# A planned attention and gated-MLP kernel: weight blocks in slice order, and new lengths in its planner

## The chip, the cores and the metric

The kernel runs on one core of one Trainium2 chip, and nothing else runs beside it. The metric is the time of one execution in microseconds (us), taken on the device; lower is better. Times of the planner stand in nanoseconds (ns), as in the code. The core's engines are called PE (matrix products), ACT, DVE and POOL in the profile's rows; SP only issues transfers. In the kernel's code PE, A, V, G and Q stand for PE, ACT, DVE, POOL and the queue that SP feeds.

## The reference

Attention in a band of 128 keys with 16 places for sink keys, of which 4 count, then a gated MLP on all heads together:

```python
batch, n_heads, seq, head_dim = (4, 8, 768, 64)
scores = scale * np.matmul(q, k.transpose(0, 1, 3, 2))
keep = is_sink | in_window          # pos < n_sink, or 0 <= rel < window
scores = np.where(keep, scores, -1000000000.0)
a = np.exp(scores - np.max(scores, axis=-1, keepdims=True))
a = a / (np.sum(a, axis=-1, keepdims=True) + 1e-09)
x = np.matmul(a, v)                 # then (B * S, H * D) = (3072, 512)
gate = 1.0 / (1.0 + np.exp(-(x @ w_gate)))      # w_gate, w_val: 512 x 1536
val = x @ w_val
out = gate * val @ w_out                        # w_out: 1536 x 512
```

The three weights are 64-bit floats on the host. They reach the chip as 64-bit words and are made into 32-bit floats there; the other arrays are 32-bit.

## The kernel before

**Attention.** A unit is one head, one batch and a stretch of 256 rows; there are 96 of them. A unit loads its q and k (`qkT`) and v (`vraw`, `vhl`), multiplies scores, masks and reduces them on DVE (`top`), takes the exponential on ACT (`exp`), scales by the sum (`share`, `mul` or `scale`, whichever engine takes it), turns the weights over on PE (`turn`), masks them into two parts on POOL (`split`, `rest_of`) and multiplies with v (`pv`). The first 20 units (`PLAIN`) do this in plain 32-bit products, the other 76 with numbers that are split into a high and a low half, so that PE can run its faster format. Four PSUM buffers (tag "a") serve the scores, the turned weights and the outputs of all units; an output of a plain unit stays in such a buffer until it has been copied out.

**The MLP.** The 12 stretches of 256 rows of x are grouped in 8 chunks, the last four of two stretches each ("pairs", which save products by sums of blocks). For every chunk the kernel goes through 12 slices of 128 of the 1536 inner columns: products with gate and value weights, tanh on ACT, product of both on DVE, split into `gh` and `gl`, and the product with the output weight, summed in PSUM. Chunk 0 (`feed_whole`) takes the decoded 32-bit weights as they are. While it runs, `halves` splits each weight block into a high half, which stays, and a low half, which `spare` writes to DRAM (`wlo_d`); `fetch` reads these back for all later chunks. `thirds` makes three more halves of each slice for the pairs.

**Weights.** For every slice `weights` loads three blocks of 128 x 512 64-bit numbers, 512 KB each (gate, value, output), through three buffers (`wst`), and `decode` makes 32-bit numbers of each with two steps on ACT (the second may go to DVE or POOL) and two on DVE. Gate and value blocks are cut out of 512 x 1536 matrices: each partition gets four rows of 1 KB. An output block has 4 KB in one row for each partition. Nothing is fetched from `wlo_d` before all blocks are decoded (`DECODED`).

**The order of the work.** Every step is written down as `plan.op(priority, ways, reads, writes)`, where `ways` lists the engines that could do it with the time in ns that the step would hold each of them. `Plan.run` plays the whole kernel through with these times when the kernel is built, gives each engine that comes free the ready step of lowest priority number (PE takes first what has been ready for a while, `SURE`), chooses buffers, and writes the instructions of each engine in the order so found. On the chip each engine works off its list in that order, whatever the real times are, and waits where an input is late. `LAT` (180 ns) is the time from a step's end to the start of a step on another engine that needs it, `NEXT` that on the same engine, `BULK`, 650 and 750 are parts of a transfer's time, `Port` marks steps of DVE and POOL that hold each other up. Until 130 us the planner puts in filler products (`warm`) where PE would otherwise be idle too long.

**The end.** Whether the fast path was valid is counted on the chip, and a branch at the end skips `general`, a slow path. `hint` places an instruction on PE, DVE and SP ahead of that branch that names its likely target; it stands in the last slice of the last chunk (`last_slice`).

## Time and profile before

| | |
|---|---|
| median of 3 runs | 771.19 us (770.46 to 771.49) |
| the profiled execution | 774.19 us |
| its span, first to last instruction | 772.5 us |
| busy: PE, DVE, ACT, POOL | 749.1, 607.5, 472.0, 506.1 us |
| mean granted clock of PE | 0.998 of 2.4 GHz |
| transfers | 184.45 MB, 75.9% of the 16 DMA engines' span |

The span lies 1.7 us under the profiled execution's own time, and that is 3.0 us over the median of the runs. "Busy" counts the time from an instruction's start to its modelled end, so that of two products that overlap in the pipeline the common part counts once. A share over the whole span is a mean over stages that differ; the rows further down take them apart.

### The profile page before, as it was taken

The page shows a single profiled execution, that of the slowest core. Times are in us where ns is not written, and L with a number is a line of the kernel's source. Part 1 is how long each engine was busy: PE and PEld are TensorE (multiplying, and loading weights), DVE is VectorE, ACT ScalarE, POOL GpSimd, SP SyncE. Part 2 cuts the span into 40 slices and gives each one's busy share as a digit, 9 for nine tenths or more (in the row PEclk, how much of TensorE's full clock was granted, in tenths as well). Part 3 has the DMA queues.
Part 4 walks back from the last instruction along what each step waited for, and adds up shares of the span by engine and source line. Part 5 has one row for each costly group of instructions (what it writes and reads, how often), then busy time and mean ns, then how long its engine had stood idle before and what let it go on. Part 6 is the DMA issues. An engine that isn't in the chain of part 4 may idle for free.

```text
span 772.5 us, 16296 instructions
## 1 busy us (share of the span) xinstructions
PE 749.1 (97%) x4986; PEld 674.9 (87%) x4986; DVE 607.5 (79%) x1782; ACT 472.0 (61%) x1338; POOL 506.1 (66%) x647
## 2 busy tenths in 40 slices
PE   7999999999999999999999999999999999999995
PEld 6866777998989999989999988999999999999995
DVE  5979988996999999969988889778999884433333
ACT  7879888765765777737666665457776652322221
POOL 3654676887999999937777977557976855321210
PEclk9999999999999999999999999999999999999999
DMA  6898987999999877677767777867697655677662
GB/s 165 222 297 250 323 263 234 376 307 311 342 294 319 284 220 207 200 252 231 233 224 225 242 233 222 246 196 251 193 306 249 196 159 178 217 240 211 198 205 86
DMA packets 120879, 185.57 MB, mean 240 GB/s; under 512 B 23248, under 2 KB 45264, under 8 KB 120784
## 3 DMA queue, kind: packets, MB, share of 16 engines
q1 hardware_dynamic: 120784, 184.45, 75.9%
q8 instruction: 42, 0.69, 0.4%
q14 instruction: 53, 0.43, 0.2%
HBM read 159.24 MB, written 25.17 MB: 239 GB/s over the span
## 4 chain that ended last, share of the span: by engine, by line
PE 61%; DVE 11%; DMA 6%; POOL 3%; ACT 2%; issue 2%; SPq 0%; ACTq 0%; POOLq 0%; DVEq 0%
PE m L620 34%; PE a L620 16%; PE o L620 11%; DVE ws L620 2%; DMA wst<-in_moe_w_gate_dram 1%; DMA out_dram<-w 1%; DVE P L620 1%; DVE th L620 1%; DMA vraw<-in_vt_dram 1%; DMA lo<-wlo_d 1%; DVE vhl L620 1%; POOL wt L620 1%; DVE hi L620 1%; DVE gl L620 1%; DVE xf L620 1%
## 5 line engine op out<-in xcount | busy, mean ns | idle before, releaser
L620 PE MATMUL m<-ws,ws 128*128 128x256 f32 x1536 | 290.0, 284 | 0.6 <-DVE th L620 0.2
L620 PE MATMUL m<-ws,lo 128*128 128x256 f32 x1344 | 288.6, 283 | 1.9 <-DMA lo<-wlo_d 1.3
L620 PEld LDWEIGHTS m<-ws,ws 128*128 128x128 f32 x1536 | 244.9, 189 | 13.1 <-DVE th L620 1.0
L620 PEld LDWEIGHTS m<-ws,lo 128*128 128x128 f32 x1344 | 215.0, 189 | 3.1 <-DMA lo<-wlo_d 2.3
L620 POOL TENSOR_SCALAR_AFFINE_SELECT wt<-wt 128x512 fp32r<-128x512 f32 (+3 forms) x192 | 125.9, 657 | 43.5 <-DVE wt L620 18.7
L620 POOL TENSOR_TENSOR gl<-th,gh 128x512 fp32r<-128x512 f32 (+1 forms) x34 | 38.2, 1122 | 99.6 <-ACT gh L620 82.7
L620 ACT ACTIVATE P<-P,negm_all 128x144 f32<-128x144 f32 x192 | 78.9, 412 | 28.7 <-DVE negm_all L620 26.8
L620 ACT ACTIVATE th<-m 128x256 f32<-128x256 f32 x96 | 36.6, 382 | 75.5 <-DVE th L620 71.9
L620 DVE TENSOR_TENSOR cv<-m,cv 128x256 f32<-128x256 f32 x96 | 40.2, 418 | 52.4 <-ACT cv L620 34.8
L620 ACT CAST gh<-th 128x512 fp32r<-128x512 f32 (+1 forms) x82 | 42.9, 523 | 55.3 <-DVE th L620 53.7
L620 POOL TENSOR_TENSOR ws<-ws,ws 128x512 fp32r<-128x512 f32 (+1 forms) x53 | 66.6, 1262 | 9.8 <-DVE ws L620 6.9
L620 PE MATMUL o<-ws,gh 128*128 128x512 f32 x168 | 67.6, 403 | 0.0
L620 PE MATMUL o<-ws,gl 128*128 128x512 f32 x168 | 66.2, 394 | 0.0
L620 PE MATMUL o<-lo,gh 128*128 128x512 f32 x168 | 65.8, 391 | 0.0
L620 DVE CUSTOM_DVE_ANT_0 P<-a,am 128x144 f32<-128x144 f32 x192 | 58.3, 306 | 8.8 <-PE a L620 2.2
L620 PE MATMUL a<-wt,vhl 128*128 128x256 f32 (+2 forms) x282 | 61.0, 327 | 1.8 <-POOL wt L620 1.6
L620 POOL TENSOR_TENSOR kl<-qkT,hi 128x400 fp32r<-128x400 f32 (+1 forms) x56 | 59.2, 1057 | 1.8
L620 PEld LDWEIGHTS a<-wt,vhl 128*128 128x128 f32 x282 | 47.3, 189 | 10.5 <-POOL wt L620 4.1
L620 ACT CAST hi<-qkT 128x656 fp32r<-128x656 f32 (+1 forms) x70 | 49.2, 703 | 10.9 <-PE a L620 10.0
L620 POOL TENSOR_TENSOR P<-P,rs 128x288 f32<-128x288 f32 x46 | 35.1, 764 | 29.8 <-DVE rs L620 26.2
L620 POOL TENSOR_TENSOR hi<-qkT,hi 64x256 fp32r<-64x256 f32 x53 | 41.2, 777 | 14.9 <-issue 4.9
L620 DVE COPY_PREDICATED a<-tri,a 128x128 f32<-128x128 int32 x160 | 45.4, 284 | 3.5 <-PE a L620 3.2
(146 smaller groups left out, 1735.5 us busy)
## 6 DMA issues: line engine op xcount, KB each, us to landing
lo<-wlo_d SPq DMA_DIRECT2D x396, 256.0 KB, 3.7
wlo_d<-ws SPq DMA_DIRECT2D x72, 256.0 KB, 4.3
qkT<-in_qk_dram SPq DMA_DIRECT2D x52, 328.0 KB, 4.1
qkT<-in_qk_dram SPq DMA_DIRECT2D x24, 264.0 KB, 3.5
wst<-in_moe_w_gate_dram SPq DMA_DIRECT2D x12, 512.0 KB, 4.8
wst<-in_moe_w_val_dram SPq DMA_DIRECT2D x12, 512.0 KB, 5.1
wst<-in_moe_w_out_dram SPq DMA_DIRECT2D x12, 512.0 KB, 5.4
out_dram<-w SPq DMA_DIRECT2D x20, 256.0 KB, 4.4
```

The costliest lines, as they stand in the source:

```text
L620: return lambda *a, **kw: tc.keep_in_program_order(op(*a, **kw))
```

## The change

- numpy puts the gate and value weights in the order slice, partition, block, column on the host, so that a block is loaded in rows of 4 KB; `weights` and the shapes taken from the arrays follow.
- The planner's times: ACT, POOL and some PE and DVE steps get shorter lengths; the time from a step's end to its reader is `AFTER` of the engine that did it and `TOLD` of the engine that reads, in place of `LAT`; a transfer takes `REACH` from its issue, its own time by `moved(packets, bytes)`, and `LANDED`; and the planner issues no transfer that would stand behind more than `QUEUED` ns of others.
- The eight loads of a batch's sink values write parts of a buffer, not all of it, in the planner's books.
- The copies of x of chunks 2 and 3 read `SPLIT`, which each of the 36 high halves of `halves` writes: the planner puts them behind all of these.
- `hint` is placed in the seventh slice of the last chunk (`NF - 6`) in place of the twelfth.

Three more hunks, each with one changed number of ns, and unchanged lines are left out.

```diff
@@ -57,13 +57,17 @@
-LAT = 180.0
-BULK = 620.0
-ISSUE = 550.0
+AFTER = dict(PE=163.0, V=75.0, A=100.0, G=35.0, Q=0.0)
+TOLD = dict(PE=54.0, V=35.0, A=35.0, G=77.0, Q=27.0)
+REACH = 1800.0
+LANDED = 600.0
+QUEUED = 4000.0
+SHARE = 1.6
+ISSUE = 480.0
...
-NEXT = dict(PE=0.0, V=60.0, A=60.0, G=60.0, Q=0.0)
+NEXT = dict(PE=0.0, V=10.0, A=25.0, G=0.0, Q=0.0)
@@ -86,6 +90,7 @@
+GUARD = 0
@@ -408,14 +413,19 @@
                     same = len(x.ways) == 1 and x.ways[0][0] == on
-                    x.ready = max(x.ready, now + (NEXT[on] if same else LAT))
+                    lat = AFTER[on] + TOLD[x.ways[0][0]]
+                    x.ready = max(x.ready, now + (NEXT[on] if same else lat))
-                        x.sure = max(x.sure, now + LAT + (SURE_D if o.dma else SURE))
+                        x.sure = max(x.sure, now + lat + (SURE_D if o.dma else SURE))
...
                 if free[e] > now:
+                    continue
+                if e == "Q" and dma_free > now + REACH + QUEUED:
+                    n += 1
+                    heapq.heappush(events, (dma_free - REACH - QUEUED, n, None))
@@ -440,7 +450,7 @@
-                        or any(slots[k][v - 1][1] + LAT + SURE > now for k, v in need.items())
+                        or any(slots[k][v - 1][1] + AFTER["V"] + TOLD["PE"] + SURE > now for k, v in need.items())
@@ -494,7 +504,7 @@
-                        port = now + ns + (70.0 if e == "V" else 0.0)
+                        port = now + ns + AFTER[e]
@@ -510,9 +520,8 @@
                     if o.dma:
-                        slow = BULK if o.dma > 1000.0 else 0.0
-                        dma_free = max(dma_free + o.dma, end + 650 + slow + o.dma)
-                        end = dma_free + 750
+                        dma_free = max(dma_free, now + REACH) + o.dma
+                        end = dma_free + LANDED
@@ -523,7 +532,7 @@
-                        x.due = max(x.due, end + LAT)
+                        x.due = max(x.due, end + AFTER[e] + TOLD[x.ways[0][0]])
@@ -561,14 +570,13 @@
-    w_gate, w_val, w_out = (
-        w.bitcast(I32).rearrange("r (c w) -> r c w", w=2) for w in (w_gate, w_val, w_out)
+    w_gate, w_val = (
+        w.bitcast(I32).rearrange("f p c (y w) -> f p c y w", w=2) for w in (w_gate, w_val)
+    w_out = w_out.bitcast(I32).rearrange("r (c w) -> r c w", w=2)
-    DM, DF, _ = w_gate.shape
+    NF, _, NC, _, _ = w_gate.shape
-    NC = DM // 128
-    NF = DF // 128
@@ -633,10 +641,13 @@
     def act(cols, psum=False):
-        return 120 + 0.9 * cols
+        return 28 + 0.93 * cols
     def pool(cols):
-        return Port(170 + 2.17 * cols)
+        return Port(135 + 2.17 * cols)
+
+    def moved(n, size):
+        return n * (9 + size / 27.0 + SHARE * size / 160.0)
@@ -836,7 +847,7 @@
-    WLO, LOADS, GROUPS, DECODED, READY, READY2 = (Fixed(None) for _ in range(6))
+    WLO, SPLIT, GROUPS, DECODED, READY, READY2 = (Fixed(None) for _ in range(6))
@@ -851,7 +862,7 @@
-                        u + 0.5, 91.0, lambda x=x, y=y, o=o: Q.dma_start(
+                        u + 0.5, moved(4, 256), lambda x=x, y=y, o=o: Q.dma_start(
@@ -862,9 +873,9 @@
-                u, 91.0, lambda o=o: Q.dma_start(
+                u, moved(8, 256), lambda o=o: Q.dma_start(
-                ), [READY2], [(raw, o)] + [VSHL[b, i] for i in range(2) if b and (b, i) in VSHL],
+                ), [READY2], [(raw, o)] + [(VSHL[b, i], o) for i in range(2) if b and (b, i) in VSHL],
@@ -880,11 +891,11 @@
-            u, 0.75 * n * R / D, lambda: Q.dma_start(out=qkT()[0:R, 0:n], in_=qk[b, h, 0:R, c0 : c0 + n]),
+            u, moved(R // 16, 4 * n), lambda: Q.dma_start(out=qkT()[0:R, 0:n], in_=qk[b, h, 0:R, c0 : c0 + n]),
...
-            u, 100.0 * L, lambda: Q.dma_start(
+            u, moved(8 * L, 256) if plain else moved(8, 256 * L), lambda: Q.dma_start(
@@ -969,12 +980,12 @@
-            plan.op(u, [("PE", 10 + (4 * n / 2.4 + 6 if plain else 2 * mac(n)), scores)], qk_reads, [sc, (P, t)], busy=0.5 if plain else 0.9)
+            plan.op(u, [("PE", (10 + 4 * n / 2.4 + 6 if plain else 249 if n > 256 else 177), scores)], qk_reads, [sc, (P, t)], busy=0.5 if plain else 0.9)
-                u, [("V", 260 if first else 535, top)],
+                u, [("V", 222 if first else 545, top)],
-            plan.op(u, [("A", 410, exp)], [], [(P, t), (rs, t)])
+            plan.op(u, [("A", 405, exp)], [], [(P, t), (rs, t)])
@@ -1000,16 +1011,16 @@
-                ("A", 200, lambda: A.activation(
+                ("A", 100, lambda: A.activation(
-                ("G", Port(213), guard(G)), ("V", Port(100), guard(V)),
+                ("G", Port(178), guard(G)), ("V", Port(75), guard(V)),
...
-            u, [("V", 110, lambda: V.reciprocal(out=rs()[:, 0:T], in_=rs()[:, 0:T]))], [], [rs]
-        )
-        plan.op(u, [("G", Port(660), share), ("A", 720, mul), ("V", Port(555), scale)], [rs], [P])
+            u, [("V", 75, lambda: V.reciprocal(out=rs()[:, 0:T], in_=rs()[:, 0:T]))], [], [rs]
+        )
+        plan.op(u, [("G", Port(621), share), ("A", 625, mul), ("V", Port(555), scale)], [rs], [P])
@@ -1070,7 +1081,7 @@
-        plan.op(u, [("PE", 30 + (T + plain) * 110, turn)], [P], [tp, wt], busy=0.45)
+        plan.op(u, [("PE", 20 + T * 60 + 190 * plain, turn)], [P], [tp, wt], busy=0.45)
@@ -1082,8 +1093,8 @@
-        plan.op(u, [("G", Port(180 + 0.9 * Z * (T - f) * 128), split)], [], [wt])
-        plan.op(u, [("G", Port(180 + 0.9 * Z * T * 128), rest_of)], [], [wt])
+        plan.op(u, [("G", Port(145 + 0.9 * Z * (T - f) * 128), split)], [], [wt])
+        plan.op(u, [("G", Port(145 + 0.9 * Z * T * 128), rest_of)], [], [wt])
@@ -1208,7 +1219,7 @@
                 hi, lo = lambda: H1()[:, i], lambda: L1()[:, i]
-                copy(u, W, hi, xv, read, [(H1, i), (L1, i)], plain)
+                copy(u, W, hi, xv, read + [SPLIT] * (ci > WHOLE + GUARD), [(H1, i), (L1, i)], plain)
@@ -1260,7 +1271,7 @@
-        plan.op(prio, [("Q", ISSUE, lambda: Q.dma_start(out=st(), in_=src))], [], [st], dma=1456.0)
+        plan.op(prio, [("Q", ISSUE, lambda: Q.dma_start(out=st(), in_=src))], [], [st], dma=moved(8, 8 * n * m))
@@ -1310,7 +1321,7 @@
-            decode(prio(), w[:, fs].rearrange("(c p) f w -> p c f w", p=128), whole)
+            decode(prio(), w[f], whole)
@@ -1318,7 +1329,7 @@
-            pr, 728.0, lambda: Q.dma_start(
+            pr, moved(8, 2048), lambda: Q.dma_start(
@@ -1326,7 +1337,9 @@
         hi, lo = slot(F32R, shape), slot(F32R, shape)
-        copy(pr, 512, hi, whole, [whole, *r], [hi, (lo, 0)], start=start)
+        copy(
+            pr, 512, hi, whole, [whole, *r], [hi, (lo, 0)] + [(SPLIT, (f, k))] * (k > 2), start=start
+        )
@@ -1388,7 +1401,7 @@
-            dma(ci, 728.0, lambda ot=ot, r=r: Q.dma_start(out=out[r : r + 128], in_=ot()), [ot])
+            dma(ci, moved(8, 2048), lambda ot=ot, r=r: Q.dma_start(out=out[r : r + 128], in_=ot()), [ot])
@@ -1464,7 +1477,7 @@
-                pr, 728.0, lambda x=x, k=k: Q.dma_start(
+                pr, moved(8, 2048), lambda x=x, k=k: Q.dma_start(
@@ -1636,6 +1649,8 @@
         gh, gl = gated(pr, 512, th)
+        if ci == len(CHUNKS) - 1 and f == NF - 6:
+            hint([gh], [th], [wol])
@@ -1662,7 +1677,6 @@
-        hint([(gh, 1)], [(th, 1)], [wol])
         high = gh, (lambda: woh()[:, 0], lambda: wol())
@@ -1797,6 +1811,8 @@
+    for name in ("moe_w_gate", "moe_w_val"):
+        made[name] = inputs[name].reshape(4, 128, -1, 128).transpose(2, 1, 0, 3)
```

## Rows read from the trace of the kernel before

**Rows 1.** Busy time by stage: length, time and count for each engine, clock, DMA share, GB/s.

```profile
0.00:20.00 20.00, 14.75 (x89) 12.99 (x90) 11.33 (x65) 15.05 (x45) 6.86 (x23) 1.00 0.64 162
20.00:140.00 120.00, 115.15 (x573) 88.61 (x572) 105.25 (x291) 104.11 (x223) 74.22 (x90) 1.00 0.89 272
140.00:340.00 200.00, 196.77 (x1386) 181.23 (x1385) 177.59 (x507) 131.30 (x412) 173.23 (x217) 1.00 0.87 283
340.00:480.00 140.00, 138.13 (x971) 128.19 (x969) 124.87 (x387) 88.85 (x274) 107.64 (x143) 1.00 0.72 228
480.00:760.00 280.00, 279.83 (x1957) 260.49 (x1956) 184.80 (x529) 130.68 (x382) 144.17 (x176) 1.00 0.69 214
760.00:772.50 12.50, 4.51 (x22) 3.39 (x20) 3.66 (x8) 2.00 (x5) 0.00 (x0) 0.87 0.24 89
```

**Rows 2.** The chain that ended last, 700 to 716 us: start, length, what.

```profile
710.80 1.43 PE m L620 x12
...
713.64 1.39 PE a L620 x6
```

**Rows 3.** Instruction groups of PE, shapes apart: count, busy us, mean ns, idle before.

```profile
L620 PE MATMUL m<-ws,ws 128*128 128x256 f32 x1536 | 290.0, 284 | 0.6 <-DVE th L620 0.2 <-ACT th L620 0.2
...
L620 PE MATMUL m<-ident 128*128 128x128 f32 x52 | 9.9, 317 | 1.4 <-POOL ident masks.py:199 1.4
```

**Rows 4.** Waits of PE: for whom, us in total, times, longest us.

```profile
PE a L620 <- POOL P L620: 3.3, 4, 1.9
PE a L620 <- POOL wt L620: 1.8, 4, 0.6
PE a L620 <- DMA qkT<-in_qk_dram: 1.6, 1, 1.6
```

**Rows 5.** Timeline of SP: first and last weight block, start and length of the issue.

```profile
8.71 0.59 SPq L620 DMA_DIRECT2D wst<-in_moe_w_gate_dram  x1
...
118.95 0.33 SPq L620 DMA_DIRECT2D wst<-in_moe_w_out_dram  x1
```

**Rows 6.** Two short stretches in the form of rows 1.

```profile
119.00:119.50 0.50, 0.50 (x2) 0.19 (x1) 0.31 (x1) 0.50 (x1) 0.00 (x0) 1.00 0.93 303
121.00:121.40 0.40, 0.40 (x3) 0.35 (x3) 0.40 (x2) 0.40 (x4) 0.04 (x1) 1.00 0.89 317
```

**Rows 7.** DMA issues of the page: count, KB each, median us from issue to landing.

```profile
lo<-wlo_d SPq DMA_DIRECT2D x396, 256.0 KB, 3.7
...
wst<-in_moe_w_gate_dram SPq DMA_DIRECT2D x12, 512.0 KB, 4.8
...
wst<-in_moe_w_out_dram SPq DMA_DIRECT2D x12, 512.0 KB, 5.4
out_dram<-w SPq DMA_DIRECT2D x20, 256.0 KB, 4.4
```

**Rows 8.** Instruction groups of POOL and ACT, shapes apart, columns as in rows 3.

```profile
L620 POOL TENSOR_SCALAR_AFFINE_SELECT wt<-wt 128x512 fp32r<-128x512 f32 x128 | 94.7, 741 | 19.5 <-DVE wt L620 14.7 <-DVE rs L620 1.4 <-ACT th L620 0.2
L620 ACT ACTIVATE P<-P,negm_all 128x144 f32<-128x144 f32 x192 | 78.9, 412 | 28.7 <-DVE negm_all L620 26.8 <-POOL wt L620 0.3
...
L620 ACT ACTIVATE th<-m 128x256 f32<-128x256 f32 x96 | 36.6, 382 | 75.5 <-DVE th L620 71.9 <-PE m L620 3.1
...
L620 POOL TENSOR_TENSOR P<-P,rs 128x288 f32<-128x288 f32 x46 | 35.1, 764 | 29.8 <-DVE rs L620 26.2 <-PE a L620 3.4
```

**Rows 9.** Waits of ACT, columns as in rows 4.

```profile
ACT w L620 <- DMA out_dram<-w: 9.1, 6, 2.7
```

**Rows 10.** Timelines of DVE and ACT: a copy of x, a high half.

```profile
93.96 0.41 DVE L620 CAST ws<-a 128x256 fp32r<-128x256 f32 x1
...
146.72 0.62 ACT L620 CAST ws<-ws 128x512 fp32r<-128x512 f32 x1
```

**Rows 11.** Timeline of SP at the end.

```profile
764.55 1.55 SPq L620 DMA_DIRECT2D out_dram<-xf  x1
```

**Rows 12.** DMA queues, 764.5 to 765.8 us: packets, MB, share of 16 engines.

```profile
q8 instruction: 1, 0.02, 5.6%
```

More of the change, by code (lines that the diff above doesn't have):

```diff
@@ L1025, in attend @@
             plan.op(
-                u, [("V", 180, lambda: V.transpose(
+                u, [("V", 160, lambda: V.transpose(
                     out=turned().rearrange("p t x -> p (t x)"),
@@ L1036, in attend @@
             plan.op(
-                u, [("G", Port(610), spread(G)), ("V", two(W), spread(V))], [turned, OWN], [sk]
+                u, [("G", Port(568), spread(G)), ("V", two(W), spread(V))], [turned, OWN], [sk]
             )
@@ L1279, in decode @@
                 )),
-                ("G", Port(1340.0), lambda: G.tensor_scalar(
+                ("G", Port(1305.0), lambda: G.tensor_scalar(
                     out=by(2), in0=by(1), scalar1=2.0**-13, scalar2=-8191.0 / 16384, op0=ALU.mult,
```

## The prediction

> **What bounds the kernel now.** I read the busy time by stage first, because the page's 97% for PE is an average. From 480 to 760 us PE stands still for 280.00 - 279.83 = 0.17 us: nothing there can be gained by another order [rows 1]. One pair slice in that stage is a fixed row of products at 1.43 / 12 = 0.119 us each and of output steps at 1.39 / 6 = 0.232 us each [rows 2]. Both rates are the same everywhere, and the change alters neither the count of the products nor their tiles, so PE's useful work is fixed. What can change is the time in which PE does nothing useful. The reader is to see five places [rows 1]: 5.25 us idle in the first 20 us; 4.85 us from 20 to 140; 3.23 us from 140 to 340; 1.87 us from 340 to 480; and 7.99 us from 760 to the end, after the last products. Then there are the filler products that keep PE warm, 9.9 us [rows 3]. An idle stretch costs a little more than it shows: a product counts as busy for 0.284 us [rows 3] where the next could have followed after 0.119, so each gap hides up to 0.165 us. So at most some 10 us between 20 and 480, a part of the start, and a part of the end are to be had, of 774.2 us for the profiled execution. The runs have a median 3.0 us lower (771.19 us); I make the sum on the profiled execution and carry the difference over.
>
> Who keeps PE waiting is the second view: POOL's scaling of P and its masking of wt, 5.1 us together, and one load of q and k with 1.6 us [rows 4]. The weight load path is the third: 36 blocks are issued between 8.71 and 118.95 us [rows 5], one per 3.1 us, through three buffers, so that a buffer takes 9.2 us for load and decoding. That path is slow, yet PE is 96% busy meanwhile (115.15 of 120 us) with attention and chunk 0; decoding sets PE's pace only where PE idles.
>
> **The layout.** A gate or value block is 512 KB, in 1 KB rows before and in 4 KB rows after, as the output weight's blocks are already. In a half microsecond filled with 1 KB rows the queue moved 303 GB/s at a share of 0.93; in a stretch of 4 KB rows alone 317 GB/s at 0.89 [rows 6]. At full share that is 326 and 356 GB/s, or 1.61 and 1.47 us for a block: 0.14 us saved. Eight such blocks go through each of the three buffers, so the last block could be decoded 8 x 0.14 = 1.1 us earlier. The other bound is the landing: blocks in 4 KB rows took 5.4 us from issue, gate blocks 4.8 [rows 7]; if it is the rows that make the 0.6 us, decoding ends 8 x 0.6 = 4.8 us later. I think it is the place (the output block usually stands behind the other two), and PE's own work covers 96% of the stage either way: 1.1 us becomes 0.04. I take 0 and keep -1.1 and +4.8, which hold if PE runs out of other work.
>
> The Trainium skill (DMA: Bandwidth & Descriptors, Specifications) gives 512 B as the smallest transfer for line rate, by which 1 KB rows lose nothing and the layout saves nothing; the two rates above differ by 9%, so the trace does not quite agree. By either the sum is the same, as I take 0.
>
> **The planner's lengths.** This part re-draws every engine's order, and carries nearly all that can happen. For a 256-column ACT step the planner before takes 120 + 0.9 x 256 = 350 ns, and 180 more until another engine sees it: 530. After, it is 28 + 0.93 x 256 = 266, then 100 + 35 = 135: 401. The trace shows such a step as 382 ns long [rows 8], so the new figure is the truer one, and ACT was charged about 0.13 us too much per step. Many copies may go to ACT or DVE, and with the old figure they went to DVE, which is busy 105.25 of 120 us from 20 to 140, against 104.11 for ACT, whose busy time counts the step's tail. With ACT cheaper, copies move off DVE. I take half of the 4.85 us of that stage: -2.4 us (bounds 0 and -4.85).
>
> For a 256 KB load the planner before has 550 + 650 + 728 + 750 = 2.68 us from issue to landing; after it has 1.8 + 0.84 + 0.6 = 3.24 us. The median of 396 such loads is 3.7 us, of the output's stores 4.4 us [rows 7], so loads are asked for earlier and stores are believed later. ACT now waits 9.1 us for such stores, up to 2.7 us at a time, at the chunks' ends [rows 9], with the later ACT steps queued behind it. Of the 5.1 us between 140 and 480 I take a third: -1.7 us (bounds 0 and -5.1). That a batch's sink loads are no longer planned one after another belongs to the same term. The new hold on the DMA queue (nothing is issued that would stand behind more than 4 us of transfers) acts mostly in the first 20 us, where a load of q and k stood behind weight blocks; the start also depends on filler, and I take 0 with bounds of half its idle time, -2.6 and +2.6.
>
> **The guard (SPLIT).** The copies of x of chunks 2 and 3 now wait for the last of 36 high halves. Before, the first copy of chunk 2 ran at 93.96 us; a high half of the 36 was still copied at 146.72 [rows 10]. The first two of these sums lie in PSUM, in two of the four "a" buffers, which score, transpose and output of all units share. If they are held for these 53 us, attention goes on with two. With 96 units in some 640 us about eight fall into that time, and if one ACT exponential of 0.41 us [rows 8] is no longer hidden in each, that is +3.3 us. In its favour: four weight buffers that chunk 2 took early stay free for the halves, which then end sooner. I take 0 (bounds 0 and +3.3).
>
> **The hint** moves from the last slice to five slices earlier, about 5 x 7.8 = 39 us [rows 2]. At the end the second output store's issue took 1.55 us on SP, where a usual one takes 0.33 [rows 5, 11], and in that stretch an instruction packet is in the trace [rows 12]; the last two stores are queued behind it. If the fetch falls elsewhere, 1.2 us go; if it falls on the last store, as much may come. I take half, -0.6 us (bounds -1.2 and +1.2).
>
> **Sum.** 0 - 2.4 - 1.7 + 0 + 0 - 0.6 = -4.7 us: 769.5 us for a profiled execution, 766.5 us for the median.
>
> **Rivals.** *Lengths too short (slower).* One mechanism: the new POOL figures are those of an undisturbed step. Scaling P is 621 ns and 89 until PE sees it, 710 in all, against 840 before; the trace's step is 764 ns long on average. Masking 512 columns is 145 + 0.9 x 512 = 606 and 89, 695 in all, against 821; the trace has 741 [rows 8]. So the old order kept some 80 ns in hand and the new one lacks 50. PE executes its list as written, and stands whenever a step is late. At 80 ns for each of the 76 units that use these steps that is +6 us, 777 us, if nothing else improves; it decides as soon as PE's 5.1 us of waits on POOL grow by more than the 4.7 us gained. Against it: the planner prefers for PE what has been ready for 600 ns, and it still adds the waits between POOL and DVE.
>
> The Trainium skill (SBUF — State Buffer, Who interferes with whom) has VectorE and GpSimd take a shared port for a whole instruction, so that the second waits; that would explain POOL's longer means, but no row here shows one such wait by itself.
>
> *No difference.* The old waits go and new ones of like size come, within 0.2% (1.5 us, about what a measurement of this kernel tells from no change): 771 us. For it speaks that only 10 us of idle time spread over many small gaps is at stake.
>
> *The guard costs.* As worked out, +3.3 us on an otherwise unchanged kernel: 774.5 us.
>
> *A larger gain.* All 9.95 us of idle time from 20 to 480 go: about 761 us. For it: most gaps are under 1 us and come from orders that the planner thought free of waits. Against it: loads still vary, and the planner does not know that.
>
> **How the numbers follow.** The forecast has 0.45, the larger gain 0.10, no difference 0.15, short lengths 0.25, the guard 0.05. So faster 0.55, same 0.15, slower 0.30. The likeliest case alone reaches from 762 (two thirds of the middle's idle time, and the end) to 769.5. For 8 in 10 I go from 757 (the larger gain with 2.6 us from the start and the end's 1.2) to 779 (short lengths, and a start 2.6 us worse, cut a little).
>
> **What would show it.** Layout: fewer packets under 2 KB, gate and value blocks landing in about 4.8 us or a little less, the last block issued within 2 us of 119. Lengths: ACT's busy time up and DVE's down in 20 to 140 us, PE's idle time there near 2.4 us; ACT's waits for stores well under 9 us. Short lengths would show as PE's waits on POOL above 5 us. The guard: no copy of chunk 2's x before the 36th half, and PE waiting for DVE or ACT to free "a" around 95 to 160 us. The hint: no store's issue over 1 us at the end, last products to end in less than 8.0 us. I am wrong if idle time of PE between 20 and 480 us grows, or if the granted clock, 1.00 in all full stages now, drops at the start because filler lies elsewhere.

## The result, and the profile after

The changed kernel takes 782.5 us (median of 4 runs, 781.52 to 783.01) where the kernel before took 771.34 beside it: a ratio of 1.0129 with an interval of 1.0082 to 1.0175. It is slower by some 10 us; 766.5 was forecast, with a range to 779. The profiled execution took 781.52 us, its span 779.8 us, and the granted clock is 0.998 as before, so the time is not the clock's.

The windows of the changed kernel, in the form of [rows 1]:

```profile
0.00:20.00 20.00, 14.74 (x82) 12.24 (x83) 11.54 (x62) 15.07 (x44) 6.11 (x22) 1.00 0.60 153
20.00:140.00 120.00, 113.69 (x566) 87.39 (x565) 102.04 (x293) 112.48 (x254) 85.16 (x106) 1.00 0.87 271
140.00:340.00 200.00, 195.76 (x1371) 179.53 (x1370) 164.19 (x464) 132.07 (x406) 161.65 (x207) 1.00 0.85 275
340.00:480.00 140.00, 139.12 (x973) 127.53 (x973) 126.37 (x404) 98.22 (x313) 116.15 (x155) 1.00 0.74 233
480.00:760.00 280.00, 278.52 (x1941) 258.38 (x1940) 177.35 (x504) 125.89 (x367) 137.86 (x168) 1.00 0.70 216
760.00:779.80 19.80, 12.35 (x76) 10.71 (x74) 6.47 (x14) 3.73 (x9) 1.29 (x1) 0.92 0.28 96
```

Beside [rows 1] the reader sees PE's idle time up by 1.5 us from 20 to 140 us (6.31 in place of 4.85), by 1.0 from 140 to 340 (4.24), by 1.3 from 480 to 760 (1.48), and down by 1.0 from 340 to 480. No stage explains the loss. Idle time is also not all of it, for each gap hides up to 0.165 us and filler counts as busy. Filler has grown from 9.9 to 11.2 us; PE's groups by form show 66 pieces where [rows 3] had 52:

```profile
L628 PE MATMUL m<-ident 128*128 128x128 f32 x66 | 11.2, 310 | 1.4 <-POOL ident masks.py:199 1.4
```

A sum over all gaps is therefore taken another way. Both traces hold the same 4934 products beside the filler. If each of them in the trace of before takes the median time that its kind takes from its start to the next one's, they fill some 727.5 us. (The sum depends on how kinds are told apart: with kinds by tiles and shape it is 723.5 us, by tiles alone 717.5. It is one constant for all kernels here, so only differences between kernels count.) The last of them starts at 764.12 us, so PE has *lost* 36.6 us there: idle time with its hidden part, filler and the start. In the trace of after it starts at 771.96 us: 44.5 us lost, 7.8 more. That is the span's difference (7.3) and the half microsecond that the end gained. With kinds by tiles and shape, the filler's part, from its start to the next product's, grew by 3.5 us (11.7 to 15.2) and the gaps over 150 ns by 1.3; the rest is shorter gaps and products that follow one another later. By stage it is 3.1 us from 20 to 140, 2.3 from 140 to 340 and 1.9 from 480 to 760.

PE's waits of the changed kernel, in the form of [rows 4]:

```profile
PE a L628 <- DVE xf L628: 3.1, 5, 1.6
PE a L628 <- POOL P L628: 3.1, 3, 1.9
PE a L628 <- DVE P L628: 2.4, 4, 1.3
PE o L628 <- DVE th L628: 1.8, 2, 0.9
PE o L628 <- POOL gl L628: 1.5, 1, 1.5
...
PE a L628 <- POOL wt L628: 0.7, 2, 0.4
...
PE a L628 <- DMA qkT<-in_qk_dram: 0.4, 1, 0.4
```

The waits for POOL's P and wt have gone from 5.1 to 3.8 us, those for q and k from 1.6 to 0.4. What has grown are the waits for DVE: xf, P and th make 7.3 us, 1.8 before, and all waits for DVE 9.6 us, 2.7 before. These are rows of the kernel before, in the same form:

```profile
PE o L620 <- DVE th L620: 0.8, 1, 0.8
...
PE a L620 <- DVE xf L620: 0.4, 2, 0.2
...
PE a L620 <- DVE P L620: 0.4, 2, 0.2
```

### The profile page after: what moved, and what is told of

Read it like the earlier page. It is cut to its first block, busy times and chain, and to the rows that moved or that the text cites. A ratio compares the mean times of both kernels' runs of the same rounds, so it can differ in the third digit from the quotient of the medians.

```text
span 779.8 us, 16356 instructions
## 1 busy us (share of the span) xinstructions
PE 754.2 (97%) x5000; PEld 675.8 (87%) x5000; DVE 587.9 (75%) x1734; ACT 487.5 (63%) x1389; POOL 508.2 (65%) x655
## 4 chain that ended last, share of the span: by engine, by line
PE 58%; DVE 11%; ACT 5%; POOL 5%; DMA 3%; issue 2%; SPq 1%; POOLq 0%; ACTq 0%; DVEq 0%
PE m L628 32%; PE a L628 15%; PE o L628 11%; ACT P L628 2%; DMA qkT<-in_qk_dram 2%; POOL ws L628 1%; DMA lo<-wlo_d 1%; DVE P L628 1%; DVE ws L628 1%; DVE low L628 1%; DVE xf L628 1%; POOL wt L628 1%; DVE th L628 1%; DVE a L628 1%; DVE wt L628 1%
## 5 line engine op out<-in xcount | busy, mean ns | idle before, releaser
L628 POOL TENSOR_SCALAR_AFFINE_SELECT wt<-wt 128x512 fp32r<-128x512 f32 (+3 forms) x192 | 124.2, 648 | 31.1 <-DVE wt L628 17.6
L628 POOL TENSOR_TENSOR gl<-th,gh 128x512 fp32r<-128x512 f32 (+1 forms) x43 | 48.1, 1119 | 131.9 <-ACT gh L628 120.2
L628 POOL TENSOR_TENSOR ws<-ws,ws 128x512 fp32r<-128x512 f32 (+1 forms) x60 | 70.4, 1181 | 6.0 <-ACT ws L628 4.3
L628 POOL TENSOR_TENSOR kl<-qkT,hi 128x400 fp32r<-128x400 f32 (+1 forms) x53 | 55.6, 1048 | 1.7
L628 POOL TENSOR_TENSOR hi<-qkT,hi 64x256 fp32r<-64x256 f32 x60 | 48.3, 806 | 12.6 <-issue 2.8
L628 PE MATMUL a<-ident,P 128*128 128x128 f32 (+1 forms) x212 | 42.2, 281 | 6.7 <-POOL P L628 3.1
L628 ACT ACTIVATE wst<-wst 128x512 uint16<-128x512 uint16 x35 | 47.7, 1363 | 0.6
```

Of the source, the lines that this page charges most:

```text
L628: return lambda *a, **kw: tc.keep_in_program_order(op(*a, **kw))
```

## The experiments

The kernels are numbered as they ran. Beside them the kernel before had medians of 774 to 776 us, so ratios are compared, not microseconds. Each row of the table gives the time that PE loses in the planner's own play of the order (up to its last product, filler included), the time lost on the chip (start of the last product less 727.5 us), the excess of the second over the first, and the ratio to the kernel before with its 95% interval. The column "chip" comes from the profiled execution alone, which lies up to 4.2 us off the median of its run (run 4: 772.02 and 776.22), so a few microseconds between rows there say little; the ratio is over all executions.

| run | what it is | plan | chip | excess | ratio |
|---|---|---|---|---|---|
| before | | 11.9 | 36.6 | 24.7 | 1 |
| after | the whole change | 16.5 | 44.5 | 28.0 | 1.0129 [1.0082, 1.0175] |
| 1 | before + layout | 11.9 | 34.8 | 22.9 | 0.9968 [0.9944, 0.9993] |
| 2 | after, old transfer times | 10.3 | 46.6 | 36.3 | 1.0143 [1.0094, 1.0192] |
| 3 | after, old lengths and hand-offs | 23.7 | 48.4 | 24.7 | 1.0105 [1.0078, 1.0133] |
| 4 | before + guard | 11.6 | 34.8 | 23.2 | 1.0008 [0.9988, 1.0027] |
| 5 | before, LAT 181 | 11.7 | 40.2 | 28.5 | 1.0046 [1.0019, 1.0074] |
| 6 | before, LAT 100 | 10.5 | 50.7 | 40.2 | 1.0168 [1.0109, 1.0226] |
| 7 | before, LAT 260 | 14.5 | 44.2 | 29.7 | 1.0064 [1.0030, 1.0099] |
| 8 | after, hand-offs 180 | 25.0 | 41.7 | 16.7 | 1.0028 [1.0009, 1.0046] |
| 9 | after, 180 into PE only | 24.7 | 47.5 | 22.8 | 1.0167 [1.0132, 1.0203] |
| 10 | after, 180 into the others only | 19.4 | 41.8 | 22.4 | 1.0063 [1.0036, 1.0090] |
| 11 | before + layout + hint | 11.9 | 37.3 | 25.4 | 0.9964 [0.9943, 0.9985] |
| 12 | before, LAT 110 | 12.0 | 49.4 | 37.4 | 1.0125 [1.0086, 1.0164] |
| 13 | after, hand-offs 180, SHARE 0 | 13.4 | 36.6 | 23.2 | 0.9963 [0.9939, 0.9987] |
| 14 | run 3, SHARE 0 | 13.3 | 46.2 | 32.9 | 1.0141 [1.0087, 1.0196] |
| 15 | after, SHARE 0 | 12.8 | 60.1 | 47.3 | 1.0250 [1.0187, 1.0312] |
| 16 | after, hand-offs 150, SHARE 0 | 11.8 | 44.0 | 32.2 | 1.0054 [1.0026, 1.0081] |
| 17 | run 13, hand-offs 182 | 13.6 | 34.5 | 20.9 | 0.9955 [0.9934, 0.9976] |
| 18 | run 14, LAT 181 | 13.8 | 44.5 | 30.7 | 1.0121 [1.0072, 1.0170] |

### Runs 1 to 4: one part at a time

Run 1 has only the layout (the host's transposition, the shapes and this line), run 4 only the guard.

```diff
-            decode(prio(), w[:, fs].rearrange("(c p) f w -> p c f w", p=128), whole)
+            decode(prio(), w[f], whole)
```

Run 2 is the changed kernel with the old sizes of transfers, `ISSUE` and `BULK` and without the hold on the queue; run 3 is the changed kernel with all old lengths of engine steps, `LAT` and `NEXT`. Of each the core:

```diff
-                        dma_free = max(dma_free, now + REACH) + o.dma
-                        end = dma_free + LANDED
+                        slow = BULK if o.dma > 1000.0 else 0.0
+                        dma_free = max(dma_free + o.dma, end + 650 + slow + o.dma)
+                        end = dma_free + 750
```
```diff
-                    lat = AFTER[on] + TOLD[x.ways[0][0]]
-                    x.ready = max(x.ready, now + (NEXT[on] if same else lat))
+                    x.ready = max(x.ready, now + (NEXT[on] if same else LAT))
```

> The kernel before with the new order of the gate and value weights on the host and nothing else; every engine's list is unchanged. If the layout carries the loss, this is 5 to 10 us slower than before. If the planner's new figures carry it, this is within 0.2% of before (771.3 us), and PE's idle time by stage is that of rows 1.

> The changed kernel with the old transfer model put back (180/650/750 ns steps, old transfer times, no hold on the queue); lengths, hand-offs, guard, layout and hint stay new. If the lengths that are too short carry the loss, this stays near 782 us or above. If the transfer model carries it, this falls to about before or below it: 764 to 772 us. The planner itself counts 736.7 us for this list, against 743.8 for the changed kernel and 749.7 for before.

> The changed kernel with the old lengths and hand-offs of the engines put back; the new transfer model, guard, layout and hint stay. If lengths too short carry the loss, this is near before, 768 to 774 us. If the transfer model carries it, this is the slow one, 782 us or more: the planner itself counts 764.3 us for this list, 14.6 us more than for before.

> The kernel before with only the guard: the copies of x of chunks 2 and 3 behind the 36 high halves. If the held PSUM buffers cost what the prediction gave them, 774.5 us. If they cost nothing, within 0.3% of before; the planner itself counts 749.3 us against 749.7.

The layout gained 0.3% and the guard cost nothing, so the loss is the planner's. But either half of the new times loses by itself as much as both do (1.0143, 1.0105, 1.0129): the terms don't add. The table shows two different ways to lose. With the new lengths (run 2) the planner's order looks good in its own play, 10.3 us lost, and the excess is 36.3 us. With the new transfer times (run 3) the excess is that of before, 24.7 us, and it is the play itself that loses 23.7 us, against 11.9 before.

### Runs 5 to 8: hand-offs, and how much a mere re-drawing costs

Runs 5 to 7 change one number of the kernel before; run 8 gives the changed kernel its old hand-offs.

```diff
-LAT = 180.0
+LAT = 181.0          # run 6: 100.0, run 7: 260.0, run 12: 110.0
```
```diff
-AFTER = dict(PE=163.0, V=75.0, A=100.0, G=35.0, Q=0.0)
-TOLD = dict(PE=54.0, V=35.0, A=35.0, G=77.0, Q=27.0)
+AFTER = dict(PE=90.0, V=90.0, A=90.0, G=90.0, Q=90.0)
+TOLD = dict(PE=90.0, V=90.0, A=90.0, G=90.0, Q=90.0)
-NEXT = dict(PE=0.0, V=10.0, A=25.0, G=0.0, Q=0.0)
+NEXT = dict(PE=0.0, V=60.0, A=60.0, G=60.0, Q=0.0)
```

> The kernel before with LAT 181 in place of 180 ns: a change without meaning, which all the same re-draws the planner's order (only some 69% of PE's steps and 42% of DVE's stay in one common sequence with the old order, against 62% and 33% between the kernels before and after). Theory A (the times without slack cost the 10 us): nothing in these times changed, so within 2 us of before, lost time of PE near 36.6 us. Theory B (any re-drawn order loses, because the old order is one that happened to fit the chip): 776 to 783 us, lost time of PE 41 to 47 us.

> The kernel before with LAT 100 in place of 180 ns: hand-offs as short as the trace shows them, all other lengths as before; the planner's own total is 748.4 us, against 749.7. Theory A, in the form that the hand-off's slack is what was lost: 778 to 782 us, as with all new lengths. Theory A, in the form that the engines' lengths matter: 771 to 774. Theory B: as the nudge, 776 to 783.

> The kernel before with LAT 260 in place of 180 ns: 80 ns more slack in every hand-off; the planner's own total is 752.0 us. Theory A: not slower than before, 768 to 773 us, and the lag of the chip behind the plan shrinks from 22.8 us to 20 or less. Theory B: as the nudge, 776 to 783.

> The kernel after with hand-offs of 180 ns between all engines (90 + 90) and the old NEXT, all new lengths and the new times of transfers kept; the planner's own total is 753.7 us, against 743.8. Theory A (hand-off slack): most of the loss comes back, 771 to 775 us. Theory A (lengths): 779 to 783. Theory B: some other order, 775 to 785, with no tie to the slack.

One nanosecond of `LAT` re-draws the order and costs 0.5%; the guard, which re-draws it as well, costs nothing measurable. 80 ns more margin cost 0.6% and gain nothing, against the first expectation of run 7; run 5 lies between its two cases. So the order of before is on the good side of a draw that is, by these few, some 0.5% wide, and a difference within that width says nothing about a cause. Short hand-offs lie outside it: 1.0168 with every other time as before. And the whole change with its hand-offs back at 180 ns lies near its edge: at 1.0028, and 0.6% above run 1, which has the layout too. The hand-offs of the change are not all short: out of DVE, ACT, POOL and of transfers they are 27 to 177 ns, out of PE 190 to 240. (`AFTER` also stands for how long the port between DVE and POOL is held, so run 8 has 90 ns there in place of 75 and 35, and it has the old `NEXT`; runs 6 and 12 change `LAT` alone.)

### Runs 9 to 12: where the margin is needed

```diff
-                    lat = AFTER[on] + TOLD[x.ways[0][0]]
+                    lat = 180.0 if x.ways[0][0] == "PE" else AFTER[on] + TOLD[x.ways[0][0]]
```

Run 10 has `!=`, run 11 the layout and the hint on the kernel before.

> The kernel after with 180 ns for every hand-off into PE, and the new, short times for all others; the planner's own total is 752.0 us. The theory left by the runs so far is that the chip's span is the planner's total plus a lag, and that the lag is 20 to 28 us with hand-offs of 180 ns and 36 to 45 us with short ones. If the slack is needed ahead of PE (whose list has no free place left), the lag falls to 20 to 28 us here: span 772 to 780, ratio near 1.003. If it is needed on the chains between the other engines, the lag stays at 36 or more: span 788 or more, ratio 1.02.

> The kernel after with 180 ns for every hand-off into DVE, ACT, POOL and the queue, and the new, short times into PE; the planner's own total is 746.8 us. The reverse of the run before it: slack needed ahead of PE gives a lag of 36 us or more, a span of 783 or more; slack needed between the others gives 20 to 28 us, a span of 767 to 775, which would beat the kernel before.

> The kernel before with the layout and the moved hint and nothing else: the planner's order is that of before but for the hint itself, on every engine. The layout alone had a ratio of 0.9968; if the hint's fetch of instructions was what held the second store of the end (1.55 us in place of 0.33), the end shrinks by another 0.5 to 1.2 us: ratio 0.995 to 0.997, some 2.5 to 4 us below before. If the fetch falls on another store, 0.9968 or more.

> The kernel before with LAT 110 in place of 180 ns, a second order drawn with short hand-offs; the planner's own total is 749.9 us, that of before 749.7. If the short hand-offs made the loss of the run with LAT 100, the lag is again 33 us or more, 783 to 790 us, ratio 1.01 to 1.02. If that run had only drawn a bad order, this one lies where the nudge by 1 ns lay, ratio 1.000 to 1.006.

Run 12 repeats the loss with short hand-offs in a second order (1.0125). Runs 9 and 10 do not decide where the margin is needed: by the measure of the expectations, span less the planner's total, they lag by 30.8 and 30.4 us, between the two cases, and of the 8 us between their ratios 5.3 are lost in their plans. That measure also proved poor, for the new lengths price PE's own steps 11.2 us lower in sum (721.7 us of products in the play, 732.9 before). One of these prices can be read off the chip. These are rows of PE's timeline of the changed kernel:

```profile
209.32 0.29 PE L628 MATMUL m<-ws,lo 128*128 128x256 f32 x1
...
209.68 0.28 PE L628 MATMUL m<-ws,lo 128*128 128x256 f32 x1
...
210.03 0.29 PE L628 MATMUL m<-ws,lo 128*128 128x256 f32 x1
210.16 0.38 PE L628 MATMUL a<-ident,P 128*128 128x128 f32 x2
...
210.61 0.28 PE L628 MATMUL m<-ws,lo 128*128 128x256 f32 x1
```

Three products take 0.36 us from one `ws,lo` to the next; with the two transposes of `turn` between them it is 0.58 us, so they take 0.22. The old price was 0.25 us, the new one 0.14, so here the new figure is the less true one. That is why the table goes by lost time. Run 11 shows that a long issue at the end stays when the hint stands five slices earlier: its second store's takes 1.57 us, as 1.55 in [rows 11]. In the changed kernel it is the third store's. These are rows of SP's timelines, run 11 first:

```profile
765.21 1.57 SPq L625 DMA_DIRECT2D out_dram<-xf  x1
...
772.86 1.23 SPq L628 DMA_DIRECT2D out_dram<-xf  x1
```

### Runs 13 to 18: transfers at the trace's price, and a second draw of each

`SHARE` 1.6 makes a packet of 2 KB cost the planner 9 + 75.9 + 20.5 = 105 ns; the median of such packets in the trace of before is 84 ns. Runs 13 to 16 set it to 0 (85 ns); 17 and 18 nudge runs 13 and 14.

```diff
-SHARE = 1.6
+SHARE = 0.0
```

> The kernel after with hand-offs of 180 ns and the old NEXT, and SHARE 0 in place of 1.6 (a 2 KB packet costs the planner 85 ns, as the trace's median of 84, in place of 105). In its own plan PE loses 13.4 us (idle and filler) up to its last product, against 25.0 with SHARE 1.6. So far the chip's lost time was the plan's plus 17.6 to 30 us with hand-offs of 180 ns or more, and plus 28 to 41 us with short ones. Slack and price both count: 31 to 40 us lost on the chip, ratio 0.993 to 1.004. Only re-drawing counts: 1.005 or more.

> The kernel after with the old lengths and hand-offs (the third run), and SHARE 0 in place of 1.6; in its own plan PE loses 13.3 us, against 23.7 with SHARE 1.6. If the loss of that run (ratio 1.0105, 49.2 us lost on the chip) came from the price of transfers, which made the planner put work off, 10 us come back: 38 to 40 us lost, ratio 0.998 to 1.005. If it came from the rest of the new model (when a transfer starts and lands, the hold on the queue), it stays at 1.008 or more.

> The kernel after with SHARE 0 in place of 1.6 and nothing else; in its own plan PE loses 12.8 us, against 16.5. The short hand-offs stay, so the chip's excess over the plan should be 28 to 41 us as in the other such runs: 41 to 54 us lost, ratio 1.006 to 1.022. If the price of transfers alone had made the change slow, 36 to 40 us, ratio 1.00 to 1.004.

> As the first run of this group, with hand-offs of 150 ns in place of 180; in its own plan PE loses 11.8 us. If 150 ns still have the slack, 30 to 40 us lost, ratio 0.991 to 1.004; if the excess grows steadily as the hand-offs get shorter (25 us at 180, 38 at 105), some 30 us of excess: 42 us lost, ratio 1.007.

> The thirteenth run (the change with hand-offs of 180 ns and SHARE 0, ratio 0.9963) with hand-offs of 182 ns: a change without meaning that re-draws the order (64% of PE's steps and 45% of DVE's in one common sequence with it). If slack and price carry its result, it lies within the width of a draw seen so far (0 to 0.6% between kernels that differ without meaning): 0.994 to 1.003. If that run was a lucky draw, 1.005 or more.

> The fourteenth run (old lengths, hand-offs of 180 ns, new model of transfers with SHARE 0, ratio 1.0141) with LAT 181: the same kind of nudge. If old lengths and the new transfers lose by what they are, 1.009 to 1.019 again. If both runs with old lengths had drawn badly, 1.006 or less.

Runs 13 and 17 against run 15 are the clearest pair: two orders with 180 and 182 ns (0.9963, 0.9955), and the same kernel with the short hand-offs, `NEXT` and port times of the change (1.0250, more than either case of its expectation). 150 ns lie between (1.0054), which by itself could be a draw. These are PE's waits of run 15:

```profile
PE a L628 <- POOL P L628: 5.8, 5, 2.3
PE a L628 <- ACT P L628: 4.4, 3, 2.9
PE m L628 <- DMA lo<-wlo_d: 3.4, 3, 1.9
PE a L628 <- POOL wt L628: 2.6, 7, 0.8
PE a L628 <- DVE wt L628: 1.5, 4, 0.9
```

And these are PE's waits of run 13, where the same rows are smaller and a wait for q and k is larger:

```profile
PE a L628 <- POOL P L628: 3.3, 3, 1.9
PE a L628 <- DMA qkT<-in_qk_dram: 3.2, 3, 1.3
PE a L628 <- ACT P L628: 2.8, 2, 1.8
...
PE a L628 <- POOL wt L628: 1.1, 3, 0.5
PE a L628 <- DVE wt L628: 0.9, 2, 0.6
PE m L628 <- DMA lo<-wlo_d: 0.6, 1, 0.6
```

Summed by engine, PE's waits for POOL (10.3 us against 5.7) and for DVE (7.4 against 1.5) are longer in run 15, those for ACT and for transfers are not (5.1 against 6.6, 3.4 against 3.8). DVE is the engine that tells the runs apart: PE waits 1.5 to 4.9 us for it in the kernel before and the six runs under 1.003 (1, 4, 8, 11, 13, 17), and 4.7 to 11.7 us in the changed kernel and all other runs. What makes DVE late in each has not been shown. In run 15 PE's clock adds to it. These are windows of ten microseconds of run 15:

```profile
20.00:30.00 10.00, 6.97 (x44) 5.93 (x42) 6.57 (x22) 5.95 (x19) 4.54 (x5) 0.93 0.84 228
30.00:40.00 10.00, 9.62 (x46) 8.07 (x47) 5.88 (x24) 7.72 (x22) 4.50 (x9) 0.73 0.68 206
```

PE stands for 3.03 us of the first, and in the second the granted clock is 0.73 of 2.4 GHz, that is 1.2 GHz for about half of it. In run 13 it is 1.00 over the whole stage from 20 to 140 us. By the granted clock of run 15, 0.83 from 20 to 40 us and 0.96 from 60 to 100, this costs at most some 5 us of the 23.5 that it loses more than run 13.

The price of transfers works in both directions. With margin in the hand-offs the lower price is better (0.9963 and 0.9955, against 1.0028 in run 8), though by little more than a draw; without it, it is worse (1.0250 against 1.0129). That the high price was itself a margin is my reading; no run shows it. The first case of my expectation for run 14 failed: its plan improved by 10 us and the chip kept the loss, and run 18 says that this was no bad draw.

Runs 14 and 18 hold hand-offs of 180 ns and lose over 1% all the same. From runs 13 and 17 they differ in the lengths of the engines' steps, old against new, and in the port's hold (70 ns after DVE and none after POOL, against 90 or 91 after both); runs 3 and 8 are the same pair at the higher price of transfers. Each time the new, shorter lengths are the better ones: 0.9963 and 0.9955 against 1.0141 and 1.0121, 1.0028 against 1.0105. So margin is shown to help in the hand-offs and not in the steps. Why the old lengths lose with the new transfer times, and not with the old ones, stays open. A part is PE's clock, which is below 1.00 early in runs 3, 14 and 18, in this order, where run 13 and the kernel before have 1.00; it costs at most 2 us (0.09 of 20 us):

```profile
20.00:40.00 20.00, 19.69 (x115) 17.51 (x115) 15.90 (x59) 16.39 (x48) 13.28 (x19) 0.92 0.81 222
...
20.00:40.00 20.00, 18.48 (x107) 16.12 (x106) 16.11 (x58) 14.52 (x45) 13.20 (x19) 0.94 0.80 215
...
20.00:40.00 20.00, 19.00 (x108) 16.65 (x106) 16.18 (x58) 14.27 (x44) 13.37 (x19) 0.91 0.81 224
```

The best versions, runs 1, 11, 13 and 17, lie at 0.9955 to 0.9968, and their intervals overlap. They all have the layout, so the new times have not been shown to gain anything beyond it.

## Why the prediction was wrong

**The step that failed** is in the term "the planner's lengths", -2.4 us: I took it that a truer figure draws a better order, and that the 0.13 us by which the new planner counts an ACT step and its hand-off shorter (401 ns for 530) was an overcharge. My own row has the step at 382 ns [rows 8], so 401 leaves 19 ns for the hand-off, where the medians out of ACT in the trace of before are 33 to 77 ns by the engine that reads. Most of that 0.13 us was margin. What the runs show in its place is the price of short hand-offs: with all else of the change in place, they and the `NEXT` and port times that came with them cost some 8 us (1.0129 against 1.0028); with the old lengths, going from 180 to 100 or 110 ns costs 1.2 to 1.7% (9 to 13 us); with the change at lower packet prices they cost 2.9%. The layout hides a part of the loss: against run 1 the changed kernel is 1.6% slower. The shorter lengths of the steps, which the term also counted, did not cost anything that the runs show (runs 8, 13 and 17 against 3, 14 and 18).

The -1.7 of the transfers' lengths failed otherwise: its signs came and its gain did not. With the short hand-offs the old transfer times (run 2, 1.0143) are as slow as the new ones (1.0129).

A late step of the kind that a margin is for can be seen at 115 us. These are rows of the timelines of DVE, POOL and PE of the changed kernel, put together:

```profile
115.14 1.78 DVE L628 SCALAR_TENSOR_TENSOR ws<-wst,ws 128x512 int32<-128x512 int32 x1
116.85 0.41 DVE L628 TENSOR_TENSOR low<-a,low 64x256 f32<-64x256 f32 x1
117.18 1.15 DVE L628 TENSOR_SCALAR ws<-ws 128x512 int32<-128x512 int32 x1
118.36 0.42 DVE L628 TENSOR_TENSOR xf<-a,low 64x256 f32<-64x256 f32 x1
...
115.10 2.95 POOL L628 TENSOR_TENSOR ws<-ws,ws 128x512 fp32r<-128x512 f32 x2
...
118.93 0.36 PE L628 MATMUL a<-hi 128*128 128x272 f32 x1 [1.63 <-DVE xf L628]
```

The first DVE step takes 1.78 us and the third 1.15, while POOL is at work until 118.05; of the 35 steps of the first kind the ten with POOL idle for nine tenths of their time or more took at most 0.71 us. `xf` is late, and PE stands for 1.63 us. In the planner's play a step of the first kind takes 0.61 to 0.71 us, and only three waits of PE behind the start are longer than 0.4 us, the longest 1.04. The Trainium skill (SBUF — State Buffer, Who interferes with whom) calls the port that DVE and POOL share an exclusive lock; these rows agree with it. The change did not make such steps: the planner's price of them is the same in both kernels, and in the trace of before one took 1.51 us:

```profile
87.37 1.51 DVE L620 SCALAR_TENSOR_TENSOR ws<-wst,ws 128x512 int32<-128x512 int32 x1
```

That a hand-off of 180 ns would have covered the wait of 1.63 us has not been shown; the row shows one late step, and the ratios show what margin in all hand-offs is worth.

Part of the loss was planned, and this is the longest such wait, at 215 us, in rows of the timelines of POOL and PE of the changed kernel:

```profile
213.09 1.28 POOL L628 TENSOR_TENSOR ws<-ws,ws 128x512 fp32r<-128x512 f32 x1
214.34 0.90 POOL L628 TENSOR_TENSOR gl<-th,gh 128x256 fp32r<-128x256 f32 x1
...
213.41 0.40 PE L628 MATMUL o<-lo,gh 128*128 128x512 f32 x1
215.29 0.50 PE L628 MATMUL o<-ws,gl 128*128 128x512 f32 x1 [1.49 <-POOL gl L628]
```

The planner had put `ws` ahead of `gl` and PE's wait with it: 1.04 us in its play, 1.49 on the chip. Of the 7.9 us more that the changed kernel loses, 4.6 are the plan's (16.5 against 11.9) and 3.3 the excess (28.0 against 24.7). The excess is likely to be larger: this profiled execution of the kernel before lies 3.0 us above the median of its runs, that of the changed kernel 1.0 below. The planner's total fell by 6 us all the same (743.8 against 749.7), through the lower prices of PE's steps.

**The signs that I named for this term.** From 20 to 140 us ACT's busy time rose (104.11 to 112.48) and DVE's fell (105.25 to 102.04) as said, and PE's idle time grew there in place of halving: work moved off the busier engine and it bought nothing. ACT's waits for stores fell from 9.1 [rows 9] to 0.8 us, and loads of q and k and of low halves were hardly waited for: the transfers' part did what it should, and PE did not get that time. This is the row of the changed kernel:

```profile
ACT w L628 <- DMA out_dram<-w: 0.8, 2, 0.5
```

**The rival "lengths too short"** had the right side, at 777 us about half of the loss, and half of the mechanism: figures of an undisturbed step leave no margin. But it put this in the lengths of two POOL steps, which runs 8, 13 and 17 keep at 1.0028 and less, and PE's waits for them fell to 3.8 us instead of growing beyond 5; the waits that grew are those for DVE. It also set the planner's step with hand-off (710 and 695 ns) against the bare step of the trace (764 and 741); with the median of 54 ns from POOL to PE the lack is some 100 ns, not 50. At which hand-offs the margin was missing has not been shown, as runs 9 and 10 did not separate them.

**The layout** I took at 0 with bounds of -1.1 and +4.8 us. It is worth -0.3% (-0.5 to -4.3 us of 775), measured twice, the second time with the hint; the middle of that, 2.5 us, lies beyond my lower bound. In run 1 the last weight block is issued at 117.90 us in place of 118.95, 1.05 us earlier, close to the 1.1 that I had worked out; this is the row of its SP timeline:

```profile
117.90 0.33 SPq L625 DMA_DIRECT2D wst<-in_moe_w_out_dram  x1
```

Where the rest comes from its trace does not say. In the changed kernel the sign that I gave was hidden: that block is issued at 125.90 us, for the order around it is another. The landing is no matter of rows: in 4 KB rows gate blocks land in 4.8 us in run 1, as in 1 KB rows before, and in 5.2 in the changed kernel, whose page has these issues:

```profile
wst<-in_moe_w_gate_dram SPq DMA_DIRECT2D x12, 512.0 KB, 5.2
wst<-in_moe_w_val_dram SPq DMA_DIRECT2D x12, 512.0 KB, 4.9
wst<-in_moe_w_out_dram SPq DMA_DIRECT2D x12, 512.0 KB, 5.5
```

**The guard** at 0 was right (1.0008). The first copy of chunk 2's x is now at 157.59 us (93.96 in [rows 10]), behind the halves; the row is from DVE's timeline of the changed kernel.

```profile
157.59 0.42 DVE L628 CAST ws<-a 128x256 fp32r<-128x256 f32 x1
```

**The hint** at -0.6 was right by its size only. In the changed kernel the time from 771.96, the last product's start, to the span's end is 7.8 us, 8.4 before; but run 11 keeps the long issue with the hint moved, and in the changed kernel it falls on the third store (1.23 us), against the sign that I gave. So moving the hint does not remove it. What places it has not been shown.

**The range** ended at 779 because the slower cases were sized from POOL's 76 units. What it left out is all the other hand-offs, which the runs price together and not one by one.

## What to carry to other kernels

When a planner fixes each engine's order, the engines can't reorder and every late step is waited for; the undisturbed median is then too short a time for a hand-off. Here 180 ns did better than short ones in each combination that was run, and 260 no better. For the lengths of steps the runs do not say the same: with 180 ns between them, the shorter ones drew the better order. When such a planner's times are changed, compare lost time in its play with lost time on the chip, never its total, and nudge one number by a nanosecond first: here that alone moved the time by 0.5%. Test a layout or another fixed edit on the old order, where it is not buried under a new draw.

## What the chip showed that was not expected

DVE's `ws<-wst,ws` of 128 x 512 integers takes at most 0.71 us with POOL idle beside it and up to 1.78 us with POOL busy, two and a half times as long, and the profile books the difference as busy time, not as a wait. So DVE's busy share can overstate its work where POOL runs; it need not, for other such steps took 0.70 to 0.74 us with POOL busy all through. And in the trace of before an undisturbed hand-off takes a median of 33 to 100 ns by the pair of engines, far under the 180 of the old `LAT`; that the rest pays for late steps is what runs 6, 12 and 15 speak for.
